# Moving the Gram rows of one chunk to the last four steps of a block, two rows per step

## The chip, the cores and the metric

The kernel runs on one core of one Trainium2 chip. The metric is the device time of one execution in microseconds (us); lower is better. The timed comparisons (faster, same, slower) are made at 2% and use undisturbed ("fast") runs alone. The profiles are one execution each, with times counted from the start of their span. Engines are named PE (TensorE, matmuls), PEld (its weight loads), DVE (VectorE), ACT (ScalarE), POOL (GpSimd) and SP.

## The reference, cut to what matters

```python
# q, k, v: [4, 6080, 256]; w_in: [256, 2048]; w_out: [2048, 256]
qn = q / (norm(q, axis=1) + 1e-06)
kn = k / (norm(k, axis=1) + 1e-06)
a  = softmax(kn.transpose(0, 2, 1) @ qn / tau)   # one 256 x 256 matrix for each batch
y  = gelu_tanh((v @ a) @ w_in) @ w_out           # for all 24320 rows
```

For each batch the kernel forms a Gram matrix of q and k over all 6080 tokens and the sums of squares for the norms. From the matrix it makes `AW = a @ w_in` once per batch; then it goes through the batch in 12 blocks of 512 tokens. The Gram work of the next batch is done in small portions between the matmuls of the present one.

## The kernel before

The blocks are numbered `n` = 0 to 47, 12 to a batch, and each has eight steps `p`. A step holds four matmuls of 512 columns for `hp` with a gelu on ACT (`mm1`), and, for the block before, one "product" of eight matmuls of 256 columns (`mm2`) into one of the accumulators p, q and r. Step 7 has no product.

```python
def mm2(n, p):                      # called as mm2(n - 1, p)
    if p == 0: product(n, 1, "r", True)
    if p == 1: product(n, 5, "p", True)
    if p == 2: product(n, 2, "q", True)
    if p == 3:
        add_out(n, "q", "x1", 0, 0)              # DVE reads q
        turn(n, 0, 0, ...)                       # DVE transpose
        product(n, 3, "p", False)
    if p == 4: product(n, 6, "r", False)
    if p == 5:
        add_out(n, "r", "y53", 0, 1)             # DVE must read r ...
        product(n, 7, "r", False)                # ... before PE adds to it
    if p == 6:
        add_out(n, "r", "y5", 1, 1)
        product(n, 4, "r", False)
        turn(...); turn(...)
    if p == 7: turn(n, 1, 0, ACCS[n, "r"][:, :hc])   # frees r for the next block
```

The portions of the next batch (`nxt`) come at the end of each step. In block 1 these are the squares of the chunk, its Gram rows and its sums of squares; the chunk itself is loaded one block earlier by GpSimd's queue, each load gated by (held back until) a matmul of the step that issues it.

```python
def gram_row(b, c, i):              # two matmuls of 256 columns, for row i of chunk c
    qt, kt = qk_tiles[b, c]
    ...
for p in range(PAIRS):
    ...
    gate = mm1(n, p)
    ...
    if n == 1 and p in (0, 3):
        prep_wout(2 + p // 3)                    # weight copies on ACT
    ...
    if n >= 1:
        mm2(n - 1, p)
        if p == 1:
            sums_2(n - 1, 4, 8)
            if n == 1:
                prep_wout(4)                     # S3 = w(0,0) - w(1,0), on DVE
    if p == 5: sums_1(n)
    if p == 7: sums_2(n, 0, 4)
    if nxt < B:
        if p in (2, 5) and blk < ncn:
            load_one(nxt, blk, p // 5, gate)     # q chunk at step 2, k chunk at step 5
        c = blk - 1
        if 0 <= c < ncn:
            if p == (4 if n == 1 else 0):
                squares(nxt, c)                  # q on ACT, k on DVE
            if p >= 1 and p - 1 < len(rows_of(nxt, c)):
                gram_row(nxt, c, p - 1)          # seven rows, in steps 1 to 7
            if p == (6 if n == 1 else 3):
                sum_rows(nxt, c)                 # DVE
```

## Time and profile before

| kernel before | |
|---|---|
| time, first three runs | 721.82 us median (721.63 to 723.99) |
| time of the profiled execution | 723.49 us |
| span of the profile | 721.7 us |
| PE, DVE, ACT busy | 96%, 72%, 67% |
| PE waits in blocks 1 to 47 | 3.7 us (block 1), 0.33 us (block 2), 1.2 us (block 25) |
| granted PE clock over the span | 0.994 |

A line of a timeline gives start, duration, engine, line of the program, operation, output and inputs, shapes and count; in brackets is how long the engine had sat idle and what released it. The durations of matmuls overlap (after the change, step 1's product starts at 50.93 and lasts 1.04 us, and the next group starts at 51.81, 0.88 us behind it), so what counts is the time from one start to the next. A line of the waits gives who waited for whom, then the total, the number of times and the longest. The prediction shows the lines.

### The profile page before, as it was taken

What the parts mean: (1) busy time and instruction counts of PE and PEld (TensorE: products, weight loads), DVE (VectorE), ACT (ScalarE), POOL (GpSimd) and SP (SyncE); (2) the same over time, 40 slices, a digit from 0 to 9 for tenths busy, and PEclk for the clock granted to TensorE, in tenths of its full rate; (3) what the DMA queues carried; (4) which work ended last, traced back from release to release, by engine and by line L of the source; (5) the groups of instructions that cost most, each with busy time, mean ns of one, the idle gap of its engine ahead of it and who ended that gap; (6) DMA issues with size and microseconds to landing.
All of it is one profiled execution on the core that took longest, in us unless ns stands there. A gap on an engine that the chain in (4) does not pass through costs nothing.

```text
span 721.7 us, 12221 instructions
## 1 busy us (share of the span) xinstructions
PE 691.8 (96%) x4799; PEld 468.5 (65%) x4885; DVE 522.0 (72%) x950; ACT 486.0 (67%) x590; POOL 67.0 (9%) x125
## 2 busy tenths in 40 slices
PE   3888999999999999999999999999999999999997
PEld 2745666666666666666666666666666666666665
DVE  4586888887876888787876778888787465565565
ACT  4375766676677667766767676667667767666673
POOL 4320101100001101100000111110000000000000
PEclk9998999999999999999999999999999999999999
DMA  9996987754249788852545897674334436435122
GB/s 241 208 250 90 153 136 121 129 95 72 60 95 143 121 138 134 145 96 57 102 73 96 127 153 136 119 129 95 73 59 91 81 60 101 75 81 94 43 59 56
DMA packets 161402, 79.19 MB, mean 110 GB/s; under 512 B 150368, under 2 KB 153184, under 8 KB 160352
## 3 DMA queue, kind: packets, MB, share of 16 engines
q0 software_dynamic: 12576, 39.46, 35.0%
q1 hardware_dynamic: 147664, 37.67, 25.2%
q10 hardware_dynamic: 1104, 1.28, 0.6%
q8 instruction: 38, 0.62, 0.4%
q14 instruction: 20, 0.16, 0.1%
HBM read 78.91 MB, written 36.83 MB: 160 GB/s over the span
## 4 chain that ended last, share of the span: by engine, by line
PE 88%; DMA 6%; issue 3%; DVE 1%; POOL 1%; POOLq 0%; DVEq 0%
PE hp L450 42%; PE r L546 23%; PE p L546 11%; PE q L546 6%; DMA t<-in_k_dram 5%; PE G L213 5%; PE ps L426 1%; DMA t<-in_q_dram 1%; DVE ot L570 0%; POOL t L93 0%; DVE c L562 0%; DVE a L177 0%; DVE sq L166 0%; PE ss L237 0%; POOL vb L132 0%
## 5 line engine op out<-in xcount | busy, mean ns | idle before, releaser
L454 ACT ACTIVATE g<-hp 128x1024 bf16<-128x1024 f32 (+1 forms) x384 | 386.7, 1015 | 201.1 <-PE hp L450 184.1
L450 PE MATMUL hp<-vT,aw 128*128 128x512 bf16 (+1 forms) x1396 | 362.5, 377 | 3.1
L546 PEld LDWEIGHTS <-wcomb 128*128 128x128 bf16 x2688 | 262.9, 98 | 101.6 <-issue 6.0
L450 PEld LDWEIGHTS <-aw 128*128 128x128 bf16 x1536 | 149.8, 98 | 111.0 <-issue 2.3
L546 PE MATMUL r<-t,wcomb 128*128 128x256 bf16 (+1 forms) x1152 | 148.1, 271 | 1.0
L562 DVE TENSOR_TENSOR c<-r,y 128x256 f32<-128x256 f32 (+1 forms) x95 | 39.9, 420 | 50.7 <-PE r L546 43.1
L213 PE MATMUL G<-t 128*128 128x256 bf16 (+1 forms) x368 | 65.2, 274 | 6.5 <-DMA t<-in_k_dram 6.5
L562 DVE TENSOR_TENSOR c<-q,x 128x256 f32<-128x256 f32 (+1 forms) x48 | 20.2, 420 | 62.9 <-PE q L546 58.6
L530 DVE TENSOR_TENSOR t<-t,g 128x1024 bf16<-128x1024 bf16 (+1 forms) x96 | 65.1, 678 | 0.0
L529 DVE TENSOR_TENSOR t<-g 128x1024 bf16<-128x1024 bf16 (+1 forms) x96 | 64.9, 676 | 0.0
L528 DVE TENSOR_TENSOR t<-g,t 128x1024 bf16<-128x1024 bf16 (+1 forms) x96 | 63.3, 659 | 0.4
L570 DVE STREAM_TRANSPOSE ot<-c 128x256 f32<-128x256 f32 (+1 forms) x144 | 57.6, 425 | 1.9 <-DVE c L562 0.2
L132 POOL DMA_DIRECT2D vb<-in_v_dram x46 | 23.6, 512 | 375.2 <-PE hp L450 375.2
L517 DVE TENSOR_TENSOR t<-g 128x2048 bf16<-128x2048 bf16 (+1 forms) x48 | 57.8, 1204 | 0.0
L546 PE MATMUL q<-g,wcomb 128*128 128x256 bf16 (+1 forms) x384 | 50.2, 274 | 0.0
L546 PE MATMUL r<-g,wcomb 128*128 128x256 bf16 (+1 forms) x384 | 49.3, 271 | 0.9 <-DVE ot L570 0.3
L165 ACT ACTIVATE sq<-t 128x1792 bf16<-128x1792 bf16 (+3 forms) x26 | 43.1, 1657 | 9.7 <-DMA t<-in_q_dram 9.7
L546 PE MATMUL p<-g,wcomb 128*128 128x256 bf16 (+1 forms) x384 | 49.3, 271 | 0.1
L546 PE MATMUL p<-t,wcomb 128*128 128x256 bf16 (+1 forms) x384 | 49.3, 271 | 0.0
L213 PEld LDWEIGHTS <-t 128*128 128x128 bf16 (+1 forms) x368 | 35.7, 98 | 16.0 <-issue 7.5
L570 DVE STREAM_TRANSPOSE ot<-r 128x256 f32<-128x256 f32 (+1 forms) x48 | 21.4, 445 | 30.6 <-PE r L546 30.6
L166 DVE TENSOR_TENSOR sq<-t 128x1792 bf16<-128x1792 bf16 (+4 forms) x27 | 28.2, 1044 | 14.4 <-DMA t<-in_k_dram 11.0
(110 smaller groups left out, 343.7 us busy)
## 6 DMA issues: line engine op xcount, KB each, us to landing
out_dram<-ot SPq DMA_DIRECT2D x176, 128.0 KB, 2.4
vb<-in_v_dram POOLq DMA_DIRECT2D x42, 256.0 KB, 4.7
t<-in_q_dram POOLq DMA_DIRECT2D x19, 448.0 KB, 5.4
t<-in_k_dram POOLq DMA_DIRECT2D x19, 448.0 KB, 4.9
wst<-in_moe_w_out_dram POOLq DMA_DIRECT2D x2, 1024.0 KB, 10.5
t<-in_q_dram POOLq DMA_DIRECT2D x3, 512.0 KB, 15.2
t<-in_k_dram POOLq DMA_DIRECT2D x3, 512.0 KB, 17.1
out_dram<-ot SPq DMA_DIRECT2D x12, 112.0 KB, 4.9
```

The costliest lines, as they stand in the source:

```text
L165: nc.scalar.activation(sq[:, 0:n, 0:256], qt[:, 0:n, :], AF.Square)
L166: nc.vector.tensor_mul(sq[:, 0:n, 256:512], kt[:, 0:n, :], kt[:, 0:n, :])
L213: nc.tensor.matmul(G[b][:, jc, :], lhsT=qt[:np_, r, jc * 128 : jc * 128 + 128], rhs=kt[:np_, r, :], start=first and jc == 0, stop=last and ...
L450: mm = nc.tensor.matmul(hp[:, u, :cols], lhsT=AW[b][:, cc, fc * 128 : fc * 128 + 128], rhs=vt_tiles[n][:, cc, :cols], start=cc == 0, stop= ...
L454: nc.scalar.activation(GS[n][:, 2 * p : 2 * p + 2, :cols], hp[:, :, :cols], AF.Gelu_apprx_tanh)
L517: nc.vector.tensor_sub(t1[:, :, :hc], quarter(n, 0, 1), quarter(n, 0, 0))
L528: nc.vector.tensor_sub(v[2], b22, v[1])
L529: nc.vector.tensor_sub(v[3], b22, quarter(n, 0, 1, f0, f1))
L530: nc.vector.tensor_sub(v[4], v[2], quarter(n, 1, 0, f0, f1))
L546: nc.tensor.matmul(ACCS[n, acc][:, :hc], lhsT=wcomb[:, w, fc, :], rhs=x, start=first and fc == 0, stop=fc == 7, skip_group_check=True)
L562: nc.vector.tensor_add(CS[n][:, tj, ci, :hc], ACCS[n, acc][:, :hc], XS[n, name][:, :hc])
L570: nc.vector.transpose(OT[n][:, tj * nb : tj * nb + nb, ci, :], src.rearrange("p (x t) -> p x t", t=32))
```

## The change

Gram row 0 of batch 1 comes in step 1 of block 1, when its k chunk has not landed. The intent is to ask for the chunk later: the seven rows go into steps 4 to 7, two at a time.

```diff
-                        if p >= 1 and p - 1 < len(rows_of(nxt, c)):
-                            gram_row(nxt, c, p - 1)
+                        rows = (2 * p - 8, 2 * p - 7) if n == 1 else (p - 1,)
+                        for i in rows:
+                            if 0 <= i < len(rows_of(nxt, c)):
+                                gram_row(nxt, c, i)
```

## The prediction

> **What bounds the kernel now.** I read the page first. TensorE (PE) is busy 96% of the span, and its row of slices dips only at the start, the end and, in the clock row, once in slice 3 (54 to 72 us):
>
> ```profile
> PE   3888999999999999999999999999999999999997
> PEclk9998999999999999999999999999999999999999
> ```
>
> So elsewhere PE paces the kernel, and the change lies in the one place where its clock dips: block 1, which runs from about 48.4 to 69.4 us. Next I read the waits between 50 and 80 us. PE has two of them:
>
> ```profile
> PE G L213 <- DMA t<-in_k_dram: 3.7, 1, 3.7
> ...
> PE r L546 <- DVE ot L570: 0.3, 1, 0.3
> ```
>
> The first is Gram row 0 of batch 1, in step 1 of block 1, waiting for the first k chunk. The timeline of PE shows where it sits and what follows:
>
> ```profile
> 50.97 1.04 PE L546 MATMUL p<-t,wcomb 128*128 128x256 bf16 x8
> 55.74 0.58 PE L213 MATMUL G<-t 128*128 128x256 bf16 x2 [3.73 <-DMA t<-in_k_dram]
> 56.12 1.91 PE L450 MATMUL hp<-vT_pe,aw 128*128 128x512 bf16 x4
> 57.83 1.91 PE L546 MATMUL q<-g,wcomb 128*128 128x256 bf16 x8
> 59.53 0.63 PE L213 MATMUL G<-t 128*128 128x256 bf16 x2
> 61.41 1.04 PE L546 MATMUL p<-g,wcomb 128*128 128x256 bf16 x8
> ```
>
> Four 512-column matmuls take 1.71 us from start to start (56.12 to 57.83); in an undisturbed step they take 0.87 (62.50 to 63.37 in the same timeline). So the wait also costs speed afterwards. The windows view (busy time of PE, PEld, DVE, ACT, POOL, then granted clock, DMA share, GB/s) gives the clock:
>
> ```profile
> 53.00:54.00 1.00, 0.00 (x0) 0.00 (x0) 1.00 (x3) 0.00 (x0) 0.00 (x0) 1.00 1.55 77
> 56.00:57.00 1.00, 1.00 (x5) 0.37 (x4) 1.00 (x2) 0.00 (x0) 0.00 (x0) 0.50 1.44 221
> 62.00:63.00 1.00, 1.00 (x10) 0.70 (x8) 0.00 (x0) 1.00 (x2) 0.00 (x0) 1.00 0.85 168
> ```
>
> In windows of 0.1 us it halves at 54.36 and is whole again at 61.12. The third thing to read is what stands behind PE: VectorE (DVE). It works without a gap from 47.83 to 57.53, and its timeline then has:
>
> ```profile
> 56.31 1.22 DVE L506 TENSOR_TENSOR wcomb<-wst 128x1024 bf16<-128x1024 f32 x1
> 59.85 0.42 DVE L562 TENSOR_TENSOR c<-q,x 128x256 f32<-128x256 f32 x1 [2.32 <-PE q L546]
> 60.30 0.45 DVE L570 STREAM_TRANSPOSE ot<-c 128x256 f32<-128x256 f32 x1
> 63.61 1.09 DVE L166 TENSOR_TENSOR sq<-t 128x1792 bf16<-128x1792 bf16 x1 [2.86 <-ACT wcomb L504]
> 64.62 0.41 DVE L562 TENSOR_TENSOR c<-r,y 128x256 f32<-128x256 f32 x1
> 64.96 1.21 DVE L517 TENSOR_TENSOR t<-g 128x2048 bf16<-128x2048 bf16 x1
> 66.40 0.42 DVE L562 TENSOR_TENSOR c<-r,y 128x256 f32<-128x256 f32 x1 [0.23 <-PE r L546]
> ...
> 70.31 0.44 DVE L570 STREAM_TRANSPOSE ot<-r 128x256 f32<-128x256 f32 x1
> ```
>
> Its slack here is 2.32 + 2.86 + 0.23 us. If PE gains more than this slack lets DVE follow, DVE becomes the limit.
>
> [...] q and then k of the chunk, issued at 42.80 and 46.26 on one queue, landed at 52.3 and 55.7, about 9.5 us after each issue.
>
> **The change part by part.** Nothing is added or removed; the instruction orders of both kernels hold 9772 rows for PE in each. Rows 0 to 6 (two matmuls each) leave steps 1 to 7 and go to steps 4 (rows 0, 1), 5 (2, 3), 6 (4, 5) and 7 (6). DVE, ScalarE (ACT) and the DMA issuers keep their orders.
>
> PE without waits. Step 1's product starts at 50.97 and is through at 51.84. From there to the first product of block 2 there are 7 groups of four 512-column matmuls (0.866 each), 5 products (0.87) and 7 Gram rows (0.218): 6.06 + 4.35 + 1.53 = 11.94 us, so 63.78. Before, that product starts at 70.80. So PE alone would gain 7.0 us: 3.9 of standing still (51.84 to 55.74), about 2.6 of half clock, 0.33 of the second wait, and small gaps.
>
> PE step by step, full clock: step 2 runs 51.84 to 53.57, step 3 to 55.3, step 4's two groups to 57.0. Row 0 is now wanted at 57.0, k is there at 55.7; rows 0 and 1 end at 57.5, step 5's hp group at 58.3. Its product (the second into r after the keep) then must wait for DVE to have read r.
>
> DVE. It is free of its backlog at 57.53, as before. By the starts above its chain then is: sum for q 57.5 (its product is long done), transpose 57.95, squares of k 58.32, sum for r at 59.32, ended 59.73. The squares waited before for ACT's last weight preparation at 62.53 to 63.58; with PE's earlier steps ACT does this at about 55.6 to 56.6, so that wait vanishes. PE's product of step 5 so starts at 59.78 and not 58.3: **a new wait of about 1.45 us**. Then DVE: the t1 difference 59.66 to 60.87, sum for r at 60.9 (product ended 60.8), and from that sum to the last transpose 3.91 us as before (66.40 to 70.31): 64.8, ended 65.22. PE has by then done step 6 (to 63.26), step 7 (to 64.34) and the first group of block 2 (to 65.2), and starts the product into r at 65.27.
>
> Gain: 70.80 - 65.27 = **5.5 us**. After this point every load is gated by PE's matmuls, and PE shows no wait over 0.3 us anywhere in the rest, so I carry the shift to the end unchanged: 721.8 - 5.5 = **716.3 us**, 0.77% less.
>
> ACT's chain needs checking: gelu of step 2 at 52.9, step 3 at 54.65, preparation 55.6, copy of p 56.55, gelu of step 4 56.8, squares of q 57.7, gelu of step 5 59.3. Each hp buffer is free before PE wants it, so ACT isn't the limit.
>
> **The rivals.**
> 1. The new DVE wait cools the clock again. For: 2.3 us of idleness was enough above. Against: before the block loop, PE stood still for 1.41 us ahead of the row at 28.79 and 0.71 us ahead of 25.48, and the granted clock was 1.00 in every microsecond from 8 to 54. It would cost about 2 us: 718.
> 2. The load is only moved into the way: the next q chunk is issued behind step 2's matmuls, so at about 53.1 instead of 58.33, while k and the two transposing loads of v still run. For: the DMA share is 0.99 or more in each microsecond from 48 to 55. Against: k is ahead of it in the same queue, and row 0 has slack. Two rows and an hp group (0.44 + 0.87) must end by DVE's 59.78, so row 0 may start as late as 58.47, 2.7 us after the present landing, at no cost. The v tile for block 2 lands at 59.4 (10.5 us after 48.91) and is wanted at 64.3[...]. If it did bite: 1 to 2 us back, 717 to 718.
> 3. DVE isn't a limit (as if it had overlapped or ended sooner): PE's full 7.0, 714.8. Against: the chain above is in order and measured item by item.
> 4. The wait was hidden anyway, and some later stage is the limit: 721 to 722. Against: no other PE wait of note follows, and the chain of work that ended last passes through this very transfer.
>
> **Range and chances.** I give my sum about three quarters, rivals 1 and 2 together a sixth, the rest little. The three runs before spread by 2.4 us (721.63 to 723.99), mostly upwards, so the range is 715.1 to 718.2. Two per cent is 14.4 us, more than twice all that can be had here, so faster by over 2% has 0.01, slower 0.01, within 2% 0.98.
>
> **What would show it.** In the profile after: no wait of a Gram row for k in block 1; the granted clock at 1.00 from 52 to 66; in PE's waits a new one of r for DVE's c of about 1.4 us near 58 to 60; DVE without gaps from 47.8 to about 65; block 2's first product into r near 65.3; then a constant shift of 5.5 us. Wrong it would be if the half clock shows again, if row 0 still waits for k near 57, if the v tile of block 2 is late, or if DVE's order makes a longer wait than 1.45 us.

## The result, and the profile after

The changed kernel takes **716.6 us** (median of 6 runs, 716.08 to 718.07) against 721.2 us (median of 6, 718.88 to 723.99) for the kernel before. The ratio is 0.994, with a 95% interval of 0.9916 to 0.9964: the same at 2%, and clearly below 1. Ratios here are the mean time of one kernel's fast runs over that of the other's of the same rounds, so not quite the ratio of the medians that are quoted. In later rounds (run 9) the ratio was 0.9929 (716.97 against 721.88, 0.9915 to 0.9942).

The page of the kernel after has no dip of the clock in slice 3:

```profile
PE   3899999999999999999999999999999999999997
PEclk9999999999999999999999999999999999999999
```

In its waits between 50 and 80 us the wait for k is gone, and one line names DVE:

```profile
PE r L546 <- DVE c L562: 1.1, 1, 1.1
```

The timeline of PE in block 1 after, from the product of step 1 to the first product of block 2:

```profile
50.93 1.04 PE L546 MATMUL p<-t,wcomb 128*128 128x256 bf16 x8
51.81 1.03 PE L450 MATMUL hp<-vT_pe,aw 128*128 128x512 bf16 x4
...
57.02 0.60 PE L213 MATMUL G<-t 128*128 128x256 bf16 x4
57.45 1.03 PE L450 MATMUL hp<-vT_pe,aw 128*128 128x512 bf16 x4
59.53 1.03 PE L546 MATMUL r<-t,wcomb 128*128 128x256 bf16 x8 [1.05 <-DVE c L562]
...
65.01 1.03 PE L546 MATMUL r<-g,wcomb 128*128 128x256 bf16 x8
```

PE goes on without a pause after step 1, asks for row 0 at 57.02 and gets it at once, and stops only ahead of step 5's product. Its clock is 1.00 in this stretch; in the windows view (busy time of PE, PEld, DVE, ACT, POOL, then clock, DMA share, GB/s) the row that was at 0.50 before reads:

```profile
56.00:57.00 1.00, 1.00 (x10) 0.80 (x9) 1.00 (x2) 1.00 (x3) 0.00 (x0) 1.00 0.32 35
```

DVE's timeline after shows whom PE waits for. There is no bracket on any of these lines: DVE has no idle time of its own up to the last transpose.

```profile
56.14 1.22 DVE L506 TENSOR_TENSOR wcomb<-wst 128x1024 bf16<-128x1024 f32 x1
57.28 0.41 DVE L562 TENSOR_TENSOR c<-q,x 128x256 f32<-128x256 f32 x1
57.73 0.45 DVE L570 STREAM_TRANSPOSE ot<-c 128x256 f32<-128x256 f32 x1
58.10 1.05 DVE L166 TENSOR_TENSOR sq<-t 128x1792 bf16<-128x1792 bf16 x1
59.07 0.41 DVE L562 TENSOR_TENSOR c<-r,y 128x256 f32<-128x256 f32 x1
...
64.52 0.44 DVE L570 STREAM_TRANSPOSE ot<-r 128x256 f32<-128x256 f32 x1
```

The sum for r ends at 59.48 and PE's product starts at 59.53; the last transpose ends at 64.96 and block 2's product starts at 65.01.

To compare runs in this stretch without the start of the kernel, I use one number, **D**: from the start of step 1's product in block 1 to the start of block 2's first product into r. It is 70.80 - 50.97 = 19.83 us before and 65.01 - 50.93 = 14.08 after, a gain of 5.75. PE's work alone in this stretch is 12.81 us (0.87 for step 1's product and the 11.94 of the prediction). Further on, the gap between the two traces stays at 5.80 up to block 24 (the same copy on ACT: 89.46 against 83.66 us, 388.17 against 382.36). In block 25 it falls to 5.4, and the spans differ by 5.4.

### The profile page after: what moved, and what is told of

The parts are those of the page before. It is cut to its first block, busy times and chain, and to the rows that moved or that the text cites. A ratio compares the mean times of both kernels' runs of the same rounds, so it can differ in the third digit from the quotient of the medians.

```text
span 716.3 us, 12307 instructions
## 1 busy us (share of the span) xinstructions
PE 693.9 (97%) x4885; PEld 467.7 (65%) x4885; DVE 521.5 (73%) x950; ACT 485.9 (68%) x590; POOL 67.1 (9%) x125
## 4 chain that ended last, share of the span: by engine, by line
PE 90%; DMA 5%; DVE 2%; issue 1%; ACT 0%; POOL 0%; DVEq 0%; POOLq 0%
PE hp L450 44%; PE r L546 23%; PE p L546 11%; PE q L546 5%; PE G L213 5%; DMA t<-in_k_dram 4%; PE ps L426 2%; DMA t<-in_q_dram 1%; DVE sq L166 0%; DVE c L562 0%; DVE ot L570 0%; PE ss L237 0%; DVE t L530 0%; DVE a L177 0%; DVE wcomb L499 0%
## 5 line engine op out<-in xcount | busy, mean ns | idle before, releaser
L450 PE MATMUL hp<-vT,aw 128*128 128x512 bf16 (+1 forms) x1472 | 370.2, 377 | 0.0
```

Source lines behind the costliest of these rows:

```text
L450: mm = nc.tensor.matmul(hp[:, u, :cols], lhsT=AW[b][:, cc, fc * 128 : fc * 128 + 128], rhs=vt_tiles[n][:, cc, :cols], start=cc == 0, stop= ...
```

## The experiments

My theory: in block 1 PE lost time twice before, by standing still and by half clock behind it; after, DVE's backlog sets the time. The rivals: only the standing still counts; grouping the rows helps by itself; the new wait is a local matter of one operation; or the spread of the runs has to do with something else. The programs of the first four runs shared one chip, the next four another, the last four a third.

### 1. The kernel before, once more (b_before_again)

No edit.

> The kernel before, unchanged, profiled a second time, because its own times spread from 718.88 to 723.99 us while the changed kernel's lie from 716.08 to 718.07. My theory: the wait for the first k chunk depends on how fast the transfers go and so varies, and the half clock behind it varies too[...]. Expected: a wait of 2.5 to 4 us in step 1 of block 1, a half-clock stretch of 0, 3.4 or 6.8 us after it, and a span that follows these. Rival: the spread is noise of the measurement or of the whole run, and wait and half clock are again 3.7 and 6.8 us whatever the time.

Measured: 720.59 us, span 718.8 against 721.7 in the first profile, D 18.57 (69.30 - 50.73). PE's timeline, and the windows view of the same run:

```profile
55.21 0.59 PE L213 MATMUL G<-t 128*128 128x256 bf16 x2 [3.45 <-DMA t<-in_k_dram]
```

```profile
57.00:58.00 1.00, 1.00 (x6) 0.54 (x5) 0.15 (x1) 0.46 (x1) 0.20 (x1) 0.50 0.68 139
59.00:60.00 1.00, 0.95 (x6) 0.52 (x6) 0.87 (x2) 0.00 (x0) 0.00 (x0) 1.00 1.01 97
```

For comparison, the two edges of the half clock in the first profile, in windows of 0.1 us:

```profile
54.30:54.40 0.10, 0.00 (x0) 0.00 (x0) 0.10 (x1) 0.00 (x0) 0.00 (x0) 0.57 6.02 23
61.10:61.20 0.10, 0.10 (x1) 0.00 (x1) 0.00 (x0) 0.00 (x0) 0.00 (x0) 0.79 1.21 215
```

The windows before and after the first of these read 1.00 and 0.50, those around the second 0.50 and 1.00. If the clock went from one value to the other in one step, a mean of 0.57 says that it was full for 0.014 us of that window and halved then, at 54.31; 0.79 puts the return at 61.14. (The prediction read 54.36 and 61.12.) That stretch is 6.83 us long. In this run the wait is nearly as long (3.45), but the half clock, read in the same way, lasted from 55.21 to 58.62 only, 3.41 us, half as long. It began 3.4 us after PE's last matmul had ended (51.77), in the first profile 2.3 us after (52.01); what sets the two edges is not shown. PE had work for 5.4 us of the longer stretch (from 55.74) and for all of the other; at a clock of 0.50 four 512-column matmuls took 1.71 us from start to start in both profiles (55.59 to 57.30 in this one), at 1.00 0.87, so half speed cost 2.7 and 1.7 us (an estimate: half of those times). With 0.3 us less of standing still, that is the whole difference in D (18.57 against 19.83). So the gain of the change depends on the run of the kernel before that it is set against. The mean clocks of the timed runs before point the same way on this chip: the fastest three (720.59, 720.67, 720.85) had 0.997, the other five (721.59 to 723.12) 0.994 to 0.996. On the two other chips the order is looser, and the slowest run there (723.0 us) had 0.998, so the half clock is not all that varies.

### 2. Filling the wait (e1_fill)

```diff
+                        if n == 1 and p == 1:
+                            warm(32)          # 32 matmuls of zeros, into an hp buffer
                         if p >= 1 and p - 1 < len(rows_of(nxt, c)):   # the kernel before
```

> The kernel before with 32 matmuls of zeros put ahead of Gram row 0 in step 1 of block 1, so that TensorE is busy while it waits for k. Theory: the wait costs twice, 3.9 us standing still and about 3 us through the half clock that follows. The filler leaves the standing still as it is and takes the half clock away: the clock stays at 1.00 and the first product into r of block 2 comes at about 67.7 us instead of 70.8, the kernel 3.1 us faster than before. Rival 1: the half clock costs nothing at the end because VectorE limits anyway: no gain. Rival 2: the filler delays row 0 or the hp buffers: slower.

Measured: 719.04 us (718.94 to 719.13), ratio to before 0.9962 (0.9947 to 0.9977), D 16.90 (67.83 - 50.93). The timeline of PE:

```profile
51.80 3.66 PE L338 MATMUL warm<-zeros_bf,ones_bf 128*128 128x256 bf16 x32
55.41 0.38 PE L213 MATMUL G<-t 128*128 128x256 bf16 x2
...
67.83 1.03 PE L546 MATMUL r<-g,wcomb 128*128 128x256 bf16 x8 [0.33 <-DVE ot L570]
```

Row 0 starts as late as before, and the clock is 1.00 throughout. Run 1 is the closest comparison: the same chip, and row 0 just as late (4.48 us after step 1's product). Against it D is 1.67 lower, half of its 3.41 us of half clock. Against the first profile of before D is 2.93 lower; 0.29 of that is an earlier row 0 (4.48 us after step 1's product instead of 4.77), so 2.64 us is what the half clock cost there. Useless work in the wait gives back about half of what the change gives. It also narrows the spread: 0.2 us over its four runs, 2.5 us over the seven of before in the same rounds. That fits with run 1: the half clock is much of what varied on this chip.

### 3. The old order without the wait (e2_other_rows)

```diff
-    def gram_row(b, c, i):
+    def gram_row(b, c, i, src=None):
-        qt, kt = qk_tiles[b, c]
+        qt, kt = qk_tiles[src or (b, c)]
 ...
-                            gram_row(nxt, c, p - 1)
+                            gram_row(nxt, c, p - 1, (0, 5) if n == 1 and p <= 3 else None)
```

Three of batch 1's rows are taken from a wrong chunk. The comparison with the reference passed nevertheless, so that it is not fine enough to see this.

> The kernel before with its order kept (one Gram row in each of steps 1 to 7), but the rows of steps 1 to 3 read a chunk of batch 0 that landed long ago; the result is wrong on purpose. Theory: only the wait matters, not how the rows are grouped: the wait and the half clock go, TensorE waits about 0.4 to 0.6 us at step 5's product for VectorE (it has two more rows behind it than the changed kernel), and block 2's first product into r comes at 65.0 to 65.3, as in the changed kernel (65.01); span about 716. Rival: grouping two rows in a step helps by itself, then this comes out 0.5 us or more slower than the changed kernel in that stage.

Measured: 716.24 us, ratio 0.9929 (0.991 to 0.9948), D 14.33 (64.90 - 50.57), clock 1.00. PE:

```profile
59.42 1.03 PE L546 MATMUL r<-t,wcomb 128*128 128x256 bf16 x8 [0.87 <-DVE c L562]
...
64.90 1.03 PE L546 MATMUL r<-g,wcomb 128*128 128x256 bf16 x8 [0.32 <-DVE ot L570]
```

This is the changed kernel's time with the old grouping (D 14.08 and, in its second profile, 14.29). The wait at step 5 was longer than I expected (0.87 for 0.4 to 0.6), but the end of the stretch came out at DVE's time. The grouping in twos has no worth of its own; the absence of the wait has.

### 4. The squares one step later (e3_squares_late)

```diff
-                        if p == (4 if n == 1 else 0):
+                        if p == (5 if n == 1 else 0):     # the changed kernel
                             squares(nxt, c)
```

> The changed kernel with the squares of the first chunk in step 5 of block 1 instead of step 4, which takes 1.0 us of VectorE's work from in front of the sum that step 5's product waits for. Theory: VectorE works without a gap from 47.8 to 65 us, and its whole backlog sets the time: the wait of 1.05 us at step 5 shrinks to under 0.2, but a wait of about 1.0 us for VectorE's last transpose appears at block 2's first product into r, which stays at 65.0 (within 0.15). No gain at the end. Rival: it is that one wait that costs: then 64.0 there, and 1.0 us off the span.

Measured: 716.04 us, ratio 0.9929 (0.9906 to 0.9951), D 14.25 (64.77 - 50.52). PE:

```profile
58.38 1.03 PE L546 MATMUL r<-t,wcomb 128*128 128x256 bf16 x8 [0.31 <-DVE c L562]
...
64.77 1.03 PE L546 MATMUL r<-g,wcomb 128*128 128x256 bf16 x8 [0.51 <-DVE ot L570]
```

The wait at step 5 shrinks to 0.31, and one of 0.51 stands at block 2's product instead (0.28 more from start to start at step 6). The sizes are not those expected (under 0.2 and about 1.0), but D does not move, as the theory said. Taking 1.0 us of work from in front of the operation that is waited for was of no use here (D 14.25 against 14.08), since the same work stood in front of the next one.

### 5. One preparation on GpSimd (e4_s3_pool)

```diff
-            nc.vector.tensor_sub(wc(S3), w_half(0, 0), w_half(1, 0))
+            nc.gpsimd.tensor_sub(wc(S3), w_half(0, 0), w_half(1, 0))   # the changed kernel
```

> The changed kernel with the last weight preparation (the difference for S3, 1.2 us on VectorE) on the idle GpSimd. I measure D, from the start of block 1's step-1 product to the start of block 2's first product into r: 19.83 us before, 14.08 changed, 12.81 for TensorE without waits. Theory: VectorE's backlog is the limit of the changed kernel, so 1.14 us less of it shows in full: the wait at step 5 is under 0.2, D about 12.9 to 13.1, the kernel 1.0 us faster than the changed one (ratio to before about 0.0015 lower). Rival 1: GpSimd takes so long over it (over 7 us) that step 5's product waits for S3 instead. Rival 2: GpSimd slows VectorE by working beside it, and D stays near 14.

Measured: 717.89 us, ratio 0.9953 (0.9932 to 0.9974), D 15.11 (65.59 - 50.48). My expectation was wrong. Of the rivals, the second came true in kind (beside GpSimd's operation one of VectorE took 3.26 us for 1.22), but D did not stay near 14: it rose by about 1 us. PE waits longer at step 5, and now at step 4 too:

```profile
56.79 0.60 PE L546 MATMUL r<-t,wcomb 128*128 128x256 bf16 x4 [0.50 <-DVE t L528]
...
60.11 1.03 PE L546 MATMUL r<-t,wcomb 128*128 128x256 bf16 x8 [1.43 <-DVE c L562]
```

The timelines of POOL and of DVE:

```profile
49.72 2.93 POOL L506 TENSOR_TENSOR wcomb<-wst 128x1024 bf16<-128x1024 f32 x1
```

```profile
49.21 1.22 DVE L497 TENSOR_TENSOR wf_a<-wf_a,wst 128x1024 f32<-128x1024 f32 x1
50.46 3.26 DVE L499 TENSOR_TENSOR wcomb<-wst,wf_a 128x1024 bf16<-128x1024 f32 x1
```

DVE saved 1.22 us and lost 2.04: the operation that began beside GpSimd's took 3.26 us for 1.22, and ended 1.07 us after GpSimd's (53.72 against 52.65). DVE's operation before that, begun at 49.21, ahead of GpSimd's (49.72), kept its 1.22 us, though the trace has GpSimd's beside it from 49.72 to 50.43. Why the one was slowed and the other not is not shown, nor whether GpSimd's operation was itself slowed: no run has it alone.

### 6. Without the sums of that chunk (e5_no_sums)

```diff
-                        if p == (6 if n == 1 else 3):
+                        if n > 1 and p == 3:              # the changed kernel
                             sum_rows(nxt, c)
```

The norms of batch 1 lack one chunk.

> The changed kernel without the sums of squares of the first chunk (2.9 us of VectorE's work in step 6, behind the sum that step 5's product waits for); the norms are wrong on purpose. Theory: two limits in a row hide each other: TensorE has already lost its time at step 5, so it now reaches block 2's product just when VectorE did; the wait of 1.05 us at step 5 stays, D falls by under 0.15 from 14.08. Rival: the total of VectorE's work is what counts, then D falls to about 12.9.

Measured: 716.4 us, ratio 0.9933 (0.9916 to 0.995), D 14.30 (64.84 - 50.54). PE:

```profile
59.42 1.03 PE L546 MATMUL r<-t,wcomb 128*128 128x256 bf16 x8 [1.33 <-DVE c L562]
...
64.84 1.04 PE L546 MATMUL r<-g,wcomb 128*128 128x256 bf16 x8
```

With 2.9 us of DVE's work gone D is the same (14.08 and 14.29 in the two profiles of the changed kernel), so the rival is refuted. PE has already lost its time at step 5.

### 7. Both (e5b_both)

The edits of 4 and 6 together.

> The changed kernel with the squares in step 5 instead of 4 and without the sums of that chunk (wrong norms on purpose). Alone, the later squares gave nothing (D 14.25). Theory: both limits are then relaxed, and TensorE's own work shows: a wait of about 0.3 us at step 5 as with the later squares alone, none at block 2's product, D 13.0 to 13.2, about 1 us less than either edit alone. Rival: something else, such as ScalarE, limits at 14: D stays there.

Measured: 715.92 us (715.3 to 717.22), ratio 0.9928 (0.9908 to 0.9948), D 13.32 (63.96 - 50.64). PE:

```profile
58.24 1.03 PE L546 MATMUL r<-t,wcomb 128*128 128x256 bf16 x8
...
63.96 1.04 PE L546 MATMUL r<-g,wcomb 128*128 128x256 bf16 x8
```

Neither edit alone changed D, both together take nearly 1 us from it. D is a little over what I expected because PE waits from start to start 0.2 us at step 5 and 0.3 at step 6 for the sums into c. There are two limits in a row, both made by DVE's backlog, and each hides the gain of easing the other. The medians do not show this at their spread (the profiled run is the slowest of the four, with a wait of 1.5 us in block 25, to which run 9 turns); the trace does.

### 8. Row 0 in step 2 (e6_row0_step2)

```diff
-                        rows = (2 * p - 8, 2 * p - 7) if n == 1 else (p - 1,)
+                        rows = (((p - 2,) if p < 7 else (5, 6)) if n == 1 else (p - 1,))
```

> The changed kernel with row 0 in step 2 of block 1, rows 1 to 4 in steps 3 to 6 and rows 5 and 6 in step 7. Theory: row 0 is then wanted about 2.6 us after the step-1 product began, k lands some 1.6 to 2.2 us later, and the wait comes back in part: D is about 14.5 if the clock stays at 1.00. Whether such a wait halves the clock is open: 1.4 us of standing still did not, 3.4 and 3.7 did for 3.4 and 6.8 us. If it does, D is 15.5 to 17.5. Rival: VectorE limits anyway and a wait of 2 us is free: D 14.1.

Measured: 718.05 us (717.19 to 720.44), ratio 0.9959 (0.9929 to 0.9989), D 15.45 (65.92 - 50.47). PE:

```profile
55.45 0.38 PE L213 MATMUL G<-t 128*128 128x256 bf16 x2 [2.20 <-DMA t<-in_k_dram]
```

The wait was 2.20 us, and the clock stayed at 1.00 in the profiled run. D is then 12.81 of work, 2.37 of standing (from start to start) and 0.27 more, nearly 1 us above the 14.5 expected; the rival, that such a wait is free (D 14.1), is refuted. One timed run of 720.44 us had a mean clock of 0.997, the value that run 1 had with its 3.4 us of half clock; the two fastest had 0.998. It has no trace, so whether 2.2 us can halve the clock stays open.

### 9. The changed kernel again, and the late chunk of block 25 (a_after_again, e7_batch3)

The changed kernel's first profile has a wait for k in block 25 that the kernel before had as well, at a smaller size. First the line of before, then that of after:

```profile
401.65 0.38 PE L213 MATMUL G<-t 128*128 128x256 bf16 x2 [1.19 <-DMA t<-in_k_dram]
```

```profile
396.24 0.38 PE L213 MATMUL G<-t 128*128 128x256 bf16 x2 [1.58 <-DMA t<-in_k_dram]
```

The 448 KB of this k chunk landed 7.6 us after the issue in the first profile of before and 8.0 us in the first after, but 4.7 us in the second of before (run 1), at the same place of the program; there PE did not wait for it.

> The changed kernel, unchanged, for comparison in the same rounds. Expected as in its first run: D about 14.1 (14.3 at most), clock at 1.00 throughout block 1, no wait of a Gram row for k there, 4.5 to 6 us faster than before. Its runs fall into two groups, near 716.2 and near 718; I expect that the slower ones hold a wait of 1.2 to 1.7 us for k in block 25 and the faster ones none. Rival: the two groups come from block 1.

(The expectation of the next run says "6 of 10 profiles"; it was 5 of the 10 until then: both first profiles and runs 5, 7 and 8.) Measured: 716.97 us (716.27 to 717.17), ratio 0.9929, D 14.29 (64.73 - 50.44). The profiled run, the slowest of its five at 717.17, had a wait of 0.9 us in block 25. Profiled runs of kernels with D of 13.3 to 14.4 took 716.05 to 716.37 us where there was no such wait (runs 3, 4 and 6) and 717.17 to 718.07 where there was one of 0.9 to 1.6 (the first profile after, run 7 and this one). So among the profiled runs the slower ones go with block 25, as expected; the other timed runs have no traces, and the runs of these rounds do not fall into two clear groups.

```diff
-                        if p == (4 if n == 1 else 0):
+                        if p == {1: 4, 25: 2}.get(n, 0):
 ...
+                        if n == 25:
+                            rows = {3: (0,), 4: (1, 2), 5: (3, 4), 6: (5,), 7: (6,)}.get(p, ())
```

> The changed kernel with the same idea in block 25, where the first k chunk of batch 3 came late in 6 of 10 profiles (a wait of 1.2 to 1.7 us): squares of that chunk in step 2 instead of 0, Gram row 0 in step 3, rows 1 and 2 in step 4, 3 and 4 in step 5, 5 in step 6, 6 in step 7. Theory: no wait for k there in any run, hence no group of slower runs from it: mean about 0.7 us lower than the changed kernel's, with the fast runs unchanged. Rival: VectorE limits there as well and gives it back: no difference, or up to 0.6 us slower.

Measured: 716.5 us (716.34 to 716.71), ratio 0.9926 (0.9913 to 0.9938). There is no wait for k in block 25, and the spread is 0.4 us. But the mean is only about 0.3 us below the changed kernel's (716.51 against 716.81), less than the 0.7 expected and little for five runs each. From step 1's product in block 25 to block 26's first product into r it takes 13.19 us, in the changed kernel 13.91 with its wait of 0.9, and 12.81 in e9_s2_act (section 10), where no wait came. So the edit costs 0.38 when the chunk is in time, of which 0.21 is this new wait for DVE:

```profile
401.49 1.03 PE L546 MATMUL r<-t,wcomb 128*128 128x256 bf16 x8 [0.21 <-DVE c L562]
```

### 10. One copy on ScalarE (e9_s2_act), and with the rows of block 25 (e10_both)

```diff
-            nc.vector.tensor_copy(wc(S2), WF[1])
+        if step == 5:
+            nc.scalar.activation(wc(S2), WF[1], AF.Copy)
 ...
                 gate = mm1(n, p)                          # the changed kernel
+                if n == 1 and p == 2:
+                    prep_wout(5)
```

> The changed kernel with the copy of the weights S2 (0.6 us on VectorE) on ScalarE ahead of its gelu of step 3 instead. Moving S3 to GpSimd failed because VectorE's neighbouring operation grew from 1.22 to 3.26 us beside it[...]. Theory: VectorE's backlog is 0.6 us shorter and shows in full: the wait at step 5 falls from 1.05 to about 0.5, D to about 13.5, 0.6 us faster than the changed kernel. Rival: ScalarE, 1.05 us later in steps 3 to 5, holds up the squares (they wait for its last preparation) or the hp buffers: D stays at 14 or more.

Measured: 715.63 us (715.51 to 717.44), ratio to before 0.992 (0.9906 to 0.9933), D 13.68 (64.14 - 50.46). PE:

```profile
58.66 1.03 PE L547 MATMUL r<-t,wcomb 128*128 128x256 bf16 x8 [0.66 <-DVE c L563]
...
64.14 1.03 PE L547 MATMUL r<-g,wcomb 128*128 128x256 bf16 x8
```

The wait is 0.66 where the changed kernel on the same chip had 1.27, and D is 0.61 lower: DVE's 0.6 us shows in full, and ScalarE had room for its 1.05 us. Beside ScalarE's copy (53.32 to 54.37) DVE's operations took 0.69 us each, as in the changed kernel on the same chip, and its preparation of 1.22 us took 1.22 beside ScalarE's next one (55.17 to 56.23).

> The changed kernel with both edits, the copy of S2 on ScalarE and the rows of block 25 later. Theory: the two gains lie in different blocks and add: about 1.2 us below the changed kernel's mean, D 13.5, no wait for k in block 25. Rival: one of them gives its gain back, then it equals the better of the two alone.

Measured: 715.93 us (715.93 to 716.17), ratio 0.9919 (0.9905 to 0.9932), D 13.71 (64.22 - 50.51), no wait for k in block 25. Against the changed kernel's mean of 716.81 its mean of 715.99 is 0.8 us lower; I expected 1.2. The mean with the copy alone (e9_s2_act) is 716.06, so the two gains do not add up in the mean. The second may buy evenness (a spread of 0.2 us against 1.9, which one run of 717.44 makes), but four runs each do not settle it. These two are the best versions found, about 0.1% below the changed kernel, with intervals against before that overlap its own.

## Why the prediction was right or wrong

The time was right: 716.6 us for a predicted 716.3, within the range, and it went the predicted way. That it came so close was partly luck: I took a gain read from one profile, of an execution of 723.49 us, from the median of three other runs (721.82). Six runs put that median at 721.2, 0.6 lower, and the gain in the medians at 4.6 us, 0.9 smaller; the two errors offset. Between the two profiled executions the gain was 5.42 us (723.49 less 718.07), near the 5.5 of the sum.

- **The wait for k goes.** Right. Row 0 was predicted to be asked for at 57.0 and came at 57.02.
- **The half clock goes with it.** Right in kind and, for the profile that I read, in size: about 2.6 us predicted, 2.64 by run 2. But I took one profile for the rule. Run 1 had 3.4 us of half clock instead of 6.8 and cost 1.7 us. That, with the late k in block 25, would account for measured ratios (0.994 and 0.9929) that stand for 4.3 and 5.1 us and not for the 5.5 predicted; the timed runs have no traces, so for them it is not shown. The edges of the half clock were misread by up to 0.05 us (run 1), which changes no sum.
- **DVE becomes the limit, with a new wait at step 5.** Right in place and cause. The wait was put at 1.45 us; it is 1.05 in the waits, which count from the modelled end of the last matmul, and 1.22 from start to start (59.53 less 58.31). The rest is that DVE stood 0.25 us earlier in this run. Block 2's product was put at 65.27 and came at 65.01. The sum carries DVE's times over, some of them from PE's half clock to full clock, and they held: the preparation at L506 took 1.22 us at a PE clock of 0.50 (56.31, before) and at 1.00 (56.14, after), the sum for q 0.42 and 0.41, its transpose 0.45 and 0.45. ACT kept out of the way as reckoned: its last preparation was put at 55.6 and came at 55.53. Runs 3 to 7 bear the cause out, and add what the prediction had not said: the two places where DVE is waited for hide each other. Its own times held the hint, since PE and DVE reach block 2's product together there (65.2 and 65.22).
- **No other wait of PE over 0.3 us in the rest.** Wrong. I took the row of waits for k (6.5 us, 4 times) to be block 1 and the start of the kernel; one of the four, 1.19 us, is in block 25. The first profile after has 1.58 there, and so 0.38 of the 5.80 us gained is lost again.
- **Rival 1, the new wait cools the clock.** Did not happen: 1.00 throughout block 1, also with 2.2 us of waiting in run 8's profile.
- **Rival 2, transfers in the way.** Did not happen in block 1: the next q chunk was issued at 53.13 (predicted 53.1), row 0 found its k, and block 2's v tile was there when wanted. (That q and k land in the order of their issue on GpSimd's queue is taken from the trace of before alone: issued at 42.80 and 46.26, landed at 52.3 and 55.7.)
- **Rival 3, DVE is no limit.** D stayed 1.3 us over PE's work; false.
- **Rival 4, the gain is lost later.** Did not happen: of 5.80 us, 5.4 reached the end. But its argument, that no other wait of note follows, was the one that failed above.

## What to carry to other kernels

Here a wait on the engine that bounds the kernel cost more than its length: behind 3.7 us of standing still the granted clock was 0.50 for 6.83 us, which cost 2.6 us more by the estimate of run 2; behind a wait of 3.45 us it was 0.50 for 3.41 us (run 1), and behind one of 2.20 us it stayed at 1.00 (run 8). Filling the wait with idle matmuls and measuring again told the two costs apart (run 2). Before a wait is removed, look at how far the next engine's backlog reaches: here the gain ended there (D 14.08 for 12.81 of PE's work), and easing only one of two places where that backlog is waited for showed nothing (D 14.25 and 14.30, with both 13.32). When a view sums waits over several times, find each of them before calling the rest free.
